# Folded Fourier mixing and channel mix: the opening laid out anew

## The chip, the cores and the metric

The kernel runs on one core of a Trainium2 chip. The metric is the device time in microseconds (us), the median of several runs. On the core, TensorE (PE, with PEld for its weight loads) multiplies matrices, VectorE (DVE) and ScalarE (ACT) compute on partitions, GpSimd (POOL) makes index tables and issues most of the loads here, and SyncE (SP) issues the stores. Each engine runs its own instructions in order.

## The reference

```python
def _attn_ref(x):                      # x: (8, 3072, 256)
    X = np.fft.fft(x, axis=1)
    X = np.fft.fft(X, axis=2)
    return X.real
def _moe_ref(x, mu_k, mu_r, w_k, w_v, w_r):   # d_model 256, d_ff 1024
    x_prev = x shifted by one row along the sequence, zeros first
    xk = mu_k * x + (1.0 - mu_k) * x_prev
    xr = mu_r * x + (1.0 - mu_r) * x_prev
    k = np.maximum(xk @ w_k, 0.0)
    v = k * k @ w_v
    r = 1.0 / (1.0 + np.exp(-(xr @ w_r)))
    return r * v
```

The output of the first function is the input of the second. All arrays are float32; the kernel works in float16 with float32 sums.

## The kernel before

There are 8 batches. The Fourier sum over the 3072 rows of a batch is split into a first stage of 96 rows on the partitions, and a second of 32 to 64. Since only the real part is wanted, x is folded with its mirror image: `fold` adds to the rows that a plain load brings (`load_p`, into an `xp` tile) the mirrored rows that a gather brings (`load_m`, into an `xm` tile, read backwards). A batch comes in two halves, h = 0 and 1; in the kernel before the first has eight slots q of 96 rows and the second nine. `load_xh` loads a half.

After the fold come, for the first batch and the first half of the second, `a_sum` (two products into one sum, evicted to tile `a`), and for the others `butterfly` on DVE and `a_item` on TensorE. `d_half` and `d_item` turn `a` into the shared tile `g_all` with the table `w_eo`, `c_item` multiplies `g_all` with the table `m_cs` into `pq`, and DVE makes `halves`, `diff` and `mix_part` (or `mix`) of it, which are the inputs of the channel mix. There a chunk of 512 tokens goes through `k_products` and a Relu eviction (`k_piece`, line 618), `square`, `v_tile`, `r_item` and `v_out`.

All tables are computed on the chip. `w_pm` comes from columns `one` (one value for each partition) and a sine on ScalarE. `m_cs` comes from some twenty DVE operations on columns `row`, from `angles` (`m_angles`, `m_wrap`) and sines (`m_sine`, two parts: tables 0 to 8 and 9 to 13, `NJ1` = 9), and `m_first` mends its first slice. `ueo`, made on GpSimd, is masked on DVE and becomes `w_eo`. `rows` makes the row numbers by which the weights are gathered, on GpSimd. `keep_busy` multiplies zeros on TensorE.

The order of the work is written out by hand and pinned on each engine (`pin_order`), so an instruction that waits holds back all that stand behind it on its engine. The opening (lines 668 to 730) handles the first batch. Then a loop of steps runs, one for each quarter of a chunk: in each step `k_piece`, the work that `at(step, ...)` put down for it, `v_tile`, `v_out` and `square`. Loads of batch 1 and the first weights are issued in `loads`, the mirrored weights in `loads_2`; all go through GpSimd's queue, in order.

PSUM has three slots of 1024 columns (`ps_w`) and two of 512 (`ps_v`), taken in turn.

Of the kernel before, what the change touches and what calls it, by code (L numbers as in the profile page):

```python
# [39 lines left out]
def kernel(  # L40
# [18 lines left out]
    NJ, NJ1 = 14, 9  # L59
# [49 lines left out]
    xm_sb = [const.tile([96, XM0 + 2049], FP16, name=f"xm{n}") for n in range(3)]  # L109
    idx_4 = const.tile([96, 4], UINT32)  # L110
# [7 lines left out]
    def load_p(b, h, q0, n):  # L118
        r = 0 if q0 == 8 else 8 * h + q0 + 1
        src = dataclasses.replace(x[b, r:r + 1, :], ap=[[32 * D, 96], [D, n], [1, D]])  # L120
        nc.gpsimd.dma_start(out=xp_t[b, h][:, q0:q0 + n], in_=src)  # L121
# [4 lines left out]
    def load_m(b, h, q0, n):  # L126
        if q0 == 8:
            o, idx = 1, idx_0[:, b:b + 1]
        elif n == 8:
            o, idx = XM0, idx_8[:, b, h:h + 1]  # L130
        else:
            o, idx = XM0 + 1024 - 256 * q0, idx_4[:, 2 * h + q0 // 4:2 * h + q0 // 4 + 1]
        gather(xm_t[b, h][:, o:o + 256 * n], x.rearrange("b (s r) d -> (b s) (r d)", r=n), idx)

    def load_xh(b, h):
        x_tiles(b, h)
        for q0, n in ((0, 8), (8, 1))[:1 + h]:
            load_p(b, h, q0, n)
            load_m(b, h, q0, n)

    def fold(b, h, q0=0, n=0):

        n = n or 8 + h
# [3 lines left out]
        o = XM0 + 1792 - 256 * q0  # L147
# [5 lines left out]
    def butterfly(b, h):  # L153
        n = 8 + h
# [53 lines left out]
    for xm in xm_sb:  # L208
        V.memset(xm[:, XM0 + 2048:XM0 + 2049], 0.0)
# [24 lines left out]

    pd_f = const.tile([P, 1], FP32)
    ueo = const.tile([P, 2, 2, 64], INT32)
    w_eo = const.tile([P, 2, 128], FP16)
    nc.gpsimd.tensor_scalar(out=pd_f, in0=pcol_i, scalar1=float(TURN) / D, scalar2=None,
                            op0=ALU.mult)
    for c in range(2):  # L240
        nc.gpsimd.tensor_scalar(out=ueo[:, :, c], in0=veo_i[:, :, c], scalar1=pd_f,
                                scalar2=0.75 * (1 - c) * TURN, op0=ALU.mult, op1=ALU.add)
    nc.gpsimd.iota(idx_8, pattern=[[S // 8, B], [-1, 2]], base=S // 8 - 1, channel_multiplier=-4)
# [12 lines left out]
    V.memset(m_cs, 0.0)  # L256
# [42 lines left out]
    for i in range(2):  # L299
# [3 lines left out]
    ts(ueo, ueo, TURN - 1, ALU.bitwise_and)  # L303
    par_i = const.tile([P, 1], INT32)
    ts(par_i, pcol_i, 1, ALU.bitwise_and)
# [4 lines left out]
    t64_i = const.tile([P, 1], INT32)  # L310
    ast = const.tile([P, 2 * NJ + 64], FP32)
    ast_i = const.tile([P, 64], INT32)
    row = {n: const.tile([P, 1], FP32, name=f"row_{n}")
           for n in ("s", "c", "z", "t", "t2", "q", "rr", "rs", "ph", "ph0", "phs", "sgn", "sg0",
                     "sgs", "to", "to0", "by")}
    ts(t64_i, pcol_i, 63, ALU.bitwise_and)
# [536 lines left out]
```

## Time and profile before

| | us |
|---|---|
| median of 3 runs | 458.45 (458.33 to 458.47) |
| profiled execution, its own time | 459.53 |
| its span, first to last instruction | 457.8 |
| PE busy | 428.6 (94%) |
| DVE busy | 363.2 (79%) |
| ACT busy | 325.1 (71%) |
| POOL busy | 61.9 (14%) |
| mean granted TensorE clock | 0.999 |

The page gives busy time by engine; most of the span lies in the loop of steps. The opening is read from the timeline: each row has the start and the length in us, engine, line, operation, output and inputs, count, and in brackets the idle time of the engine before it with what ended that. Where rows of a group are merged, the length is that of all of them, gaps within included.

### The profile page before, as it was taken

The page shows a single profiled execution, that of the slowest core. Times are in us where ns is not written, and L with a number is a line of the kernel's source. Part 1 is how long each engine was busy: PE and PEld are TensorE (multiplying, and loading weights), DVE is VectorE, ACT ScalarE, POOL GpSimd, SP SyncE. Part 2 cuts the span into 40 slices and gives each one's busy share as a digit, 9 for nine tenths or more (in the row PEclk, how much of TensorE's full clock was granted, in tenths as well). Part 3 has the DMA queues.
Part 4 walks back from the last instruction along what each step waited for, and adds up shares of the span by engine and source line. Part 5 has one row for each costly group of instructions (what it writes and reads, how often), then busy time and mean ns, then how long its engine had stood idle before and what let it go on. Part 6 is the DMA issues. An engine that isn't in the chain of part 4 may idle for free.

```text
span 457.8 us, 8433 instructions
## 1 busy us (share of the span) xinstructions
PE 428.6 (94%) x3433; PEld 307.2 (67%) x3433; DVE 363.2 (79%) x523; ACT 325.1 (71%) x369; POOL 61.9 (14%) x88
## 2 busy tenths in 40 slices
PE   3348899999999999999999999999999999999996
PEld 1234667767777777777777777777777777676764
DVE  3737999998879887898879887898879865997453
ACT  3147888777777777777777777777777777666661
POOL 7872324000400031000400030000000000000000
PEclk9999999999999999999999999999999999999999
DMA  7897566722852248222852244222222222222223
GB/s 110 129 164 122 77 140 108 156 48 69 152 127 55 69 87 178 71 52 64 149 129 54 70 87 107 70 55 63 69 64 54 70 69 48 70 68 70 71 69 93
DMA packets 35739, 40.93 MB, mean 89 GB/s; under 512 B 4082, under 2 KB 31732, under 8 KB 35700
## 3 DMA queue, kind: packets, MB, share of 16 engines
q1 hardware_dynamic: 27524, 25.05, 22.1%
q0 software_dynamic: 8016, 15.21, 21.4%
q8 instruction: 27, 0.44, 0.4%
q10 hardware_dynamic: 160, 0.13, 0.1%
q14 instruction: 12, 0.10, 0.1%
HBM read 30.41 MB, written 25.17 MB: 121 GB/s over the span
## 4 chain that ended last, share of the span: by engine, by line
PE 85%; DVE 6%; POOL 4%; issue 1%; DMA 1%; ACT 1%; POOLq 0%; DVEq 0%
PE psV L646 35%; PE psW L608 33%; PE psW L632 9%; PE psW L528 3%; PE psW L490 3%; PE psW L458 2%; DVE k L625 2%; DMA wv_sb<-in_moe_w_v_dram 1%; POOL xm L124 1%; DVE x L588 1%; DVE d L552 1%; DVE p L148 1%; POOL xp L121 1%; DVE o L656 0%; POOL wk L124 0%
## 5 line engine op out<-in xcount | busy, mean ns | idle before, releaser
L618 ACT ACTIVATE rl<-psW 128x1024 f16<-128x1024 f32 x192 | 196.0, 1023 | 97.9 <-PE psW L608 92.2
L646 PE MATMUL psV<-wv_sb,k 128*128 128x256 f16 x1536 | 199.3, 273 | 0.4 <-DVE k L625 0.2
L608 PE MATMUL psW<-x,wk 128*128 128x512 f16 (+1 forms) x776 | 196.8, 377 | 1.0 <-ACT rl L618 0.6
L646 PEld LDWEIGHTS <-k 128*128 128x128 f16 x1536 | 146.0, 98 | 28.7 <-DVE k L625 1.2
L625 DVE TENSOR_TENSOR k<-rl 128x2048 f16<-128x2048 f16 (+1 forms) x98 | 117.6, 1201 | 50.9 <-ACT rl L618 47.0
L608 PEld LDWEIGHTS <-wk 128*128 128x128 f16 x776 | 75.8, 98 | 51.3 <-issue 1.8
L656 DVE SCALAR_TENSOR_TENSOR o<-psV,r 128x512 f32<-128x512 f32 (+1 forms) x97 | 66.2, 682 | 15.5 <-PE psV L646 12.6
L577 DVE TENSOR_TENSOR x<-y,t 128x1536 f16<-128x1536 f16 x60 | 57.5, 958 | 2.1
L632 PE MATMUL psW<-wr,x 128*128 128x256 f16 x384 | 49.8, 273 | 0.0
L637 ACT ACTIVATE r<-psW 128x1024 f16<-128x1024 f32 x48 | 48.9, 1018 | 0.8 <-PE psW L632 0.8
L632 PEld LDWEIGHTS <-x 128*128 128x128 f16 x384 | 37.5, 98 | 14.6 <-issue 0.3
L121 POOL DMA_DIRECT2D xp<-in_x_dram x26 | 15.1, 580 | 200.5 <-DVE p L150 187.8
L438 ACT ACTIVATE a<-psW 128x832 f16<-128x832 f32 x31 | 26.6, 859 | 14.0 <-PE psW L475 14.0
L124 POOL DMA_INDIRECT xm<-in_x_dram,idx x26 | 30.9, 1187 | 7.8 <-issue 7.6
L438 ACT ACTIVATE pq<-psW 128x768 f16<-128x768 f32 (+5 forms) x34 | 28.6, 844 | 2.5 <-PE psW L528 2.3
L438 ACT ACTIVATE g_all<-psW 128x1024 f16<-128x1024 f32 (+3 forms) x39 | 28.1, 723 | 1.4 <-PE psW L490 1.4
L528 PEld LDWEIGHTS <-g_all 128*128 128x128 f16 (+1 forms) x233 | 15.2, 99 | 11.5 <-ACT g_all L438 3.3
L528 PE MATMUL psW<-m_cs,g_all 128*128 128x128 f16 (+2 forms) x233 | 19.2, 222 | 2.5 <-ACT g_all L438 2.3
L544 DVE TENSOR_TENSOR y<-pq 128x960 f16<-128x960 f16 (+5 forms) x38 | 18.6, 531 | 3.2 <-ACT pq L438 1.9
L148 DVE TENSOR_TENSOR p<-xp,xm 96x2048 f16<-96x2048 f16 (+3 forms) x18 | 20.8, 1155 | 0.1
L475 PEld LDWEIGHTS <-p 96*128 96x128 f16 x50 | 5.9, 130 | 22.1 <-DVE p L150 21.4
L564 DVE TENSOR_SCALAR t<-d,mu_m 128x1536 f16<-128x1536 f16 x32 | 19.7, 615 | 0.0
(118 smaller groups left out, 193.1 us busy)
## 6 DMA issues: line engine op xcount, KB each, us to landing
out_dram<-o SPq DMA_DIRECT2D x190, 128.0 KB, 2.4
xp<-in_x_dram POOLq DMA_DIRECT2D x14, 384.0 KB
xp<-in_x_dram POOLq DMA_DIRECT2D x4, 192.0 KB
wv_sb<-in_moe_w_v_dram POOLq DMA_DIRECT2D x1, 512.0 KB
xm<-in_x_dram,idx POOLq DMA_INDIRECT x26
xp<-in_x_dram POOLq DMA_DIRECT2D x8, 48.0 KB
out_dram<-o ACTq DMA_DIRECT2D x2, 64.0 KB
out_dram<-o SPq DMA_DIRECT2D x2, 64.0 KB
```

Source lines behind the costliest of these rows:

```text
L124: nc.gpsimd.indirect_dma_start(dst, None, src, bass.IndirectOffsetOnAxis(ap=idx, axis=0))
L148: V.tensor_tensor(out=p[:, q0:q0 + n], in0=xp[:, q0:q0 + n], in1=_v(xm, o + 256, [(-256, n), (-1, 256)]), op=ALU.add)
L438: nc.scalar.activation(out=out_ap, in_=in_ap, func=AF.Copy)
L528: nc.tensor.matmul(out=ps[0:m, o:o + 64 * k], lhsT=g_all[:, u, 128 * min(f, 1):128 * min(f, 1) + m], rhs=m_cs[:, f % 2, sl:sl + k], start= ...
L577: V.tensor_tensor(out=dst, in0=_v(y_t[b], 64 * (NSL * a + lo + 3 * m), [(1, n)]), in1=_v(x_t["t", a], 64 * lo, [(1, n)]), op=ALU.subtract ...
L608: nc.tensor.matmul(out=st["k", ds][:, 512 * hs + lo:512 * hs + hi], lhsT=wk_sb[m][a][:, 128 * fc:128 * fc + 128], rhs=xk[:, a, 512 * i + l ...
L618: nc.scalar.activation(out=st["rl"][:, 2 * ds:2 * ds + 2], in_=st["k", ds].rearrange("p (f t) -> p f t", f=2), func=AF.Relu, bias=0.0, sca ...
L625: V.tensor_tensor(out=k2_t[c][:, lo:hi], in0=r, in1=r, op=ALU.mult)
L632: nc.tensor.matmul(out=ps[:, 256 * tb:256 * tb + 256], lhsT=x_t[b, 1, m][:, a, 512 * i + 128 * tb: 512 * i + 128 * tb + 128], rhs=wr_sb[m] ...
L637: nc.scalar.activation(out=st["r", c], in_=ps, func=AF.Sigmoid)
L646: nc.tensor.matmul(out=st["v", tb - h][:, 256 * h:256 * h + 256], lhsT=k2_t[c][:, fc, 128 * tb:128 * tb + 128], rhs=wv_sb[:, fc], start=(f ...
L656: V.scalar_tensor_tensor(out=o.rearrange("p a b -> p (a b)")[:, 0:256 * n], in0=st["v", t0][:, 0:256 * n], scalar=16.0, in1=st["r", c][:, ...
```

## The change

The opening of the first batch is written anew, with small changes to every batch's loads:

- Loads. The first half of a batch now has nine slots and the second eight. The first batch comes by a nine-slot plain load, a one-slot gather, an eight-slot gather, an eight-slot plain load and two four-slot gathers, in place of ten transfers; the later batches by two plain loads and three gathers in place of three and three. In `a_item` and `a_sum` the second half takes slot 0 of the first half where it took its own slot 8, and batch 1 gets a one-slot `butterfly` for that.
- Index tables on GpSimd. One `ramp` replaces the ramps `k1c_i`, `kst_i` and `veo_i`; `rows` is six iotas in place of nine arithmetic operations, and all of it stands ahead of the weight gathers.
- Column constants. The DVE operations on `row` columns are replaced by memsets and ten operations on rows of one partition (`row_ramps`), which TensorE turns into eight columns by eight products with a 1x1 unit (`row_turn`), and `angle_parts`. `turn_table` becomes one operation, `m_first` one copy. The clearing of `m_cs` moves from DVE to ScalarE.
- Order. The table constants come before the first fold; the folds are of 5, 4, 4 and 4 slots. The sines of `m_cs` come in three parts, tables 0 to 4, 5 to 8 and 9 to 13 (`NJ1` = 5, `NJ2` = 9). The weights are loaded before batch 1. `diff` and `mix_part` are of four slices each, and the first `k_products` stand before `c_item` of slices 9 to 16, which uses the small PSUM slots.
- `keep_busy` is called with 14, 11, 5, 1 and 4 products in the opening, in place of one call with 2; the call with 10 at the start stays.

The diff, cut to its core:

```diff
-    NJ, NJ1 = 14, 9
+    NJ, NJ1, NJ2 = 14, 5, 9
...
-    def load_p(b, h, q0, n):
-        r = 0 if q0 == 8 else 8 * h + q0 + 1
+    def load_p(b, h):
+        r, n = 9 * h, 9 - h
         src = dataclasses.replace(x[b, r:r + 1, :], ap=[[32 * D, 96], [D, n], [1, D]])
...
-    def load_m(b, h, q0, n):
...
+    def load_m(b, h, o, n, idx):
+        gather(xm_t[b, h][:, XM0 + o:XM0 + o + 256 * n],
+               x.rearrange("b (s r) d -> (b s) (r d)", r=n), idx)
+    def load_m0(b):
+        load_m(b, 0, 2048, 1, idx_0[:, b:b + 1])
     def load_xh(b, h):
         x_tiles(b, h)
-        for q0, n in ((0, 8), (8, 1))[:1 + h]:
-            load_p(b, h, q0, n)
-            load_m(b, h, q0, n)
+        load_p(b, h)
+        if h == 0:
+            load_m0(b)
+        load_m(b, h, 0, 8, idx_8[:, b, h:h + 1])
     def fold(b, h, q0=0, n=0):
-        n = n or 8 + h
+        n = n or 9 - h
...
-        o = XM0 + 1792 - 256 * q0
+        o = XM0 + 256 * (8 - h - q0)
...
-        V.memset(xm[:, XM0 + 2048:XM0 + 2049], 0.0)
-    load_p(0, 0, 0, 4)
-    load_m(0, 0, 0, 4)
-    load_p(0, 0, 4, 4)
-    load_m(0, 0, 4, 4)
...
+        V.memset(_v(xm, XM0 + 2048, [(256, 2)]), 0.0)
+    load_p(0, 0)
+    iota(pcol_i, pattern=[[0, 1]], base=0, channel_multiplier=1)
+    iota(ramp, pattern=[[1, P]], base=0, channel_multiplier=0)
+    iota(idx_0, pattern=[[S, B]], base=S, channel_multiplier=-32)
+    iota(idx_0[0:1], pattern=[[S, B]], base=0, channel_multiplier=0)
+    load_m0(0)
+    iota(idx_8, pattern=[[S // 8, B], [-1, 2]], base=S // 8 - 1, channel_multiplier=-4)
+    load_m(0, 0, 0, 8, idx_8[:, 0, 0:1])
...
+    load_p(0, 1)
+    load_m(0, 1, 1024, 4, idx_4[:, 0:1])
+    load_m(0, 1, 0, 4, idx_4[:, 1:2])
...
-    V.memset(m_cs, 0.0)
     mu_rows(0)
+    nc.scalar.activation(out=m_cs.rearrange("p c s t -> p (c s t)").bitcast(FP32),
+                         in_=_v(zeros.bitcast(FP32), 0, [(0, 2 * NJ), (1, 64)]), func=AF.Copy)
...
+    for n, v0, v1, at, v in ((PH, 0.75, 0.0, 47, 0.75), (PHS, 0.5, 0.75, 15, 0.75),
+                             (PH0, 0.75, 0.5, 47, 0.75), (PHS0, 0.5, 0.25, 15, 0.25)):
...
+    def row_ramps():
+        one = ramp[0:1]
+        ts(rv(Q, 0, (32, 4), (1, 16)), _v(one, 1, [(0, 4), (1, 16)]), 0.0, ADD)
+        ts(rv(Q, 16, (32, 4), (1, 16)), _v(one, 1, [(0, 4), (1, 16)]), 32.0, ADD)
+        V.memset(rv(Q, 15, (32, 4)), 0.0)
+        ts(rv(Q2, 0, (1, P)), rv(Q, 0, (1, P)), 2.0, MUL)
...
+    def row_turn():
+        ps = ps_w()
+        for n in range(8):
+            nc.tensor.matmul(out=ps[:, n:n + 1], lhsT=rw[:, n], rhs=unit_1, start=True, stop=True)
+        ts(cols[:, 0:TO], ps[:, 0:TO], float(TURN) / S, MUL)
+        V.tensor_copy(out=cols[:, TO:TO + 2], in_=ps[:, TO:TO + 2])
...
-    ts(row["s"], t64_i, 47.0, ALU.is_equal, 32.0, MUL)
-    ts(row["z"], t64_i, 15.0, ALU.is_equal)
-    ts(row["c"], t64_i, 32.0, ALU.is_ge, -32.0, MUL)
-    ts(row["t"], t64_i, row["c"], ADD)
...
-    ts(ast_i, kst_i[:, NJ:NJ + 64], row["rr"], MUL, float(TURN) / R, MUL)
-    ts(ast_i, ast_i, TURN - 1, ALU.bitwise_and)
-    V.tensor_copy(out=ast[:, 2 * NJ:2 * NJ + 64], in_=ast_i)
-    for i, ph in ((0, "ph"), (1, "phs")):
-        ts(ast[:, NJ * i:NJ * i + NJ], kst_i[:, 0:NJ], row["rs"], MUL, row[ph], ADD)
+    def angle_parts():
+        ts(ast_i, ramp[:, 0:64], col(RR), MUL)
+        ts(ast_i, ast_i, TURN - 1, ALU.bitwise_and)
+        V.tensor_copy(out=ast[:, 2 * NJ:2 * NJ + 64], in_=ast_i)
+        for i in range(2):
+            ts(ast[:, NJ * i:NJ * i + NJ], ramp[:, 0:NJ], col(Q2), MUL, col(PH + i), ADD)
+        V.tensor_copy(out=_v(ast[hi64], 0, [(NJ, 2)]), in_=cols[hi64, PH0:PH0 + 2])
     def turn_table():
-        ts(row["to0"], row["c"], 2.0, MUL, row["s"], ADD)
-        ts(row["to"], row["z"], -32.0, MUL, row["to0"], ADD)
...
-        ts(turn, kst_i[:, NJ:NJ + 128], row["to0"], ALU.is_equal, row["sg0"], MUL)
+        ts(turn, ramp, col(TO), ALU.is_equal, col(SG), MUL)
...
     def rows():
-        late, low, f128 = [const.tile([P, 1], FP32, name=f"row{n}") for n in range(3)]
-        ts = nc.gpsimd.tensor_scalar
-        ts(out=late, in0=pcol_f, scalar1=64.0, scalar2=-127.0, op0=ALU.is_ge, op1=ALU.mult)
-        ts(out=low, in0=pcol_f, scalar1=2.0, scalar2=late, op0=ALU.mult, op1=ALU.add)
-        ts(out=row_i[:, 0:1], in0=low, scalar1=0.0, scalar2=None, op0=ALU.add)
...
+        for a in range(2):
+            for half in range(2):
+                iota(_v(row_i[64 * half:64 * half + 64], a, [(3 - 2 * a, 2)]), pattern=[[0, 2]],
+                     base=256 * a + half * (1 - 2 * a), channel_multiplier=2 - 4 * a)
+        iota(row_i[0:1, 2:3], pattern=[[0, 1]], base=0, channel_multiplier=0)
+        iota(_v(row_i[0:1], 1, [(2, 2)]), pattern=[[0, 2]], base=128, channel_multiplier=0)
...
     def m_first():
-        im = slice(96, 128)
-        nc.scalar.activation(out=m_cs[im, 0, 0], in_=m_cs[im, 0, 0], func=AF.Copy,
-                             scale=row["sgn"][im])
-        nc.scalar.activation(out=m_cs[hi64, 1, 0], in_=m_cs[hi64, 1, 0], func=AF.Copy,
-                             scale=row["sgs"][hi64])
-        V.memset(m_cs[hi64, :, 0, 0:1], 0.0)
+        nc.scalar.activation(out=_v(m_cs[hi64], 0, [(2 * NJ * 64, 2)]), in_=zeros[hi64, 0:2],
+                             func=AF.Copy)
     def loads():
-        load_xh(1, 0)
+        rows()
         for a in range(2):
-            next(row_part)
             gather(wk_sb[0][a], moe_w_k, row_i[:, a:a + 1])
         nc.gpsimd.dma_start(out=wv_sb, in_=moe_w_v.rearrange("(fc p) v -> p fc v", p=128))
+        load_xh(1, 0)
         for a in range(2):
             gather(wr_sb[0][a], moe_w_r, row_i[:, a:a + 1])
         load_xh(1, 1)
-        next(row_part)
...
+                for z, q, o, w in ((eo_t[b, 0], 0, 0, _v(w_pm[0:96], WA, [(1, WB)])),
+                                   (eo, 7, 1, _v(w_pm[0:96], 1, [(2, WB)]))):
+                    nc.tensor.matmul(out=_v(ps, 128 * i + o, [(2, WB)]), lhsT=z[:, q, e, :],
...
-    def a_sum(b, h, q0, eng="A", n=4):
+    def a_sum(b, h, i0, engs="A"):
...
+            n = 4 // len(engs)
+            if i % n == n - 1:
+                evac(_v(a_t[b], 8 * h + i0 + i + 1 - n, [(16, 2 * WA), (1, n)]),
+                     _v(ps, 256 * (i + 1 - n), [(1, 2 * WA), (256, n)]), engs[i // n])
...
-    def c_item(b, s0, n, eng="A", turn_late=False):
+    def c_item(b, s0, n, eng="A", turn_late=False, small=False):
-        ps = ps_w()
+        ps, bank = (ps_v(), 256) if small else (ps_w(), 512)
...
-    fold(0, 0, 0, 4)
-    a_sum(0, 0, 0)
+    keep_busy(14)
+    row_ramps()
+    row_turn()
+    angle_parts()
+    ts(ueo, ueo, TURN - 1, ALU.bitwise_and)
     eo_sine()
     eo_rest()
+    keep_busy(11)
+    fold(0, 0, 0, 5)
+    a_sum(0, 0, 0)
+    fold(0, 0, 5, 4)
+    a_sum(0, 0, 4)
+    loads()
     m_angles(0, NJ1)
-    fold(0, 0, 4, 4)
-    a_sum(0, 0, 4)
     m_wrap(0, NJ1)
+    m_sine(0, NJ1)
+    m_first()
+    mu_turn()
+    keep_busy(5)
     fold(0, 1, 0, 4)
     a_sum(0, 1, 0)
-    m_sine(0, NJ1)
-    m_first()
-    fold(0, 1, 4, 5)
-    loads()
-    a_sum(0, 1, 4, "V", 2)
-    a_sum(0, 1, 6, "A", 2)
-    mu_turn()
-    m_angles(NJ1, NJ)
+    fold(0, 1, 4, 4)
+    keep_busy(1)
+    m_angles(NJ1, NJ2)
+    a_sum(0, 1, 4, "VA")
+    m_wrap(NJ1, NJ2)
     d_half(0, 0, ps_v(), "A")
     d_half(0, 2, ps_v(), "V")
-    m_wrap(NJ1, NJ)
     c_item(0, 0, 5, "A", True)
     c_item(0, 5, 4, "A", True)
+    m_sine(NJ1, NJ2)
     d_item(0, 1)
     halves(0, 0, 5)
+    diff(0, 0, 4)
+    mix_part(0, 0, 0, 4)
     halves(0, 5, 9)
-    diff(0, 0, 8)
-    for lo, hi in ((0, 4), (4, 8)):
-        mix_part(0, 0, lo, hi)
-        if lo == 0:
-            keep_busy(2)
-            c_item(0, 9, 4, "A", True)
-            c_item(0, 13, 4, "A", True)
-            m_sine(NJ1, NJ)
-            k_products(chunks[0], 0, 0, 256)
-            k_products(chunks[0], 1, 0, 256)
+    keep_busy(4, ps_w())
+    k_products(chunks[0], 0, 0, 256)
+    k_products(chunks[0], 1, 0, 256)
+    diff(0, 4, 8)
+    mix_part(0, 0, 4, 8)
+    c_item(0, 9, 4, "A", True, True)
+    c_item(0, 13, 4, "A", True, True)
+    m_angles(NJ2, NJ)
+    m_wrap(NJ2, NJ)
+    m_sine(NJ2, NJ)
...
+    at(6, butterfly, 1, 0, 1)
```

More of the change, by code (lines that the diff above doesn't have):

```diff
@@ L108 @@
     XM0 = 257
-    xm_sb = [const.tile([96, XM0 + 2049], FP16, name=f"xm{n}") for n in range(3)]
-    idx_4 = const.tile([96, 4], UINT32)
+    xm_sb = [const.tile([96, XM0 + 2306], FP16, name=f"xm{n}") for n in range(3)]
+    idx_4 = const.tile([96, 2], UINT32)
     idx_8 = const.tile([96, B, 2], UINT32)
@@ L290 @@
                             (WA, 2, "n0", one["f2"]), (WA + 1, 2, "n2", one["f3"])):
-        ts(_v(u_w, o, [(step, NU)]), k1c_i, one[by], MUL, ph, ADD)
+        ts(_v(u_w, o, [(step, NU)]), ramp[:, 0:NU], one[by], MUL, ph, ADD)
     ts(u_w, u_w, TURN - 1, ALU.bitwise_and)
@@ L302 @@
     mu_rows(1)
[L303 to L310, printed above, removed]
     ast = const.tile([P, 2 * NJ + 64], FP32)
     ast_i = const.tile([P, 64], INT32)
[L313 to L316, printed above, removed]
```

140 lines of the change are left out of this document (54 added, 86 removed).

## The prediction

> **What bounds the kernel now.** I read the page first, then the stretches, then the opening in order of time.
>
> ```profile
> span 457.8 us, 8433 instructions
> PE 85%; DVE 6%; POOL 4%; issue 1%; DMA 1%; ACT 1%; POOLq 0%; DVEq 0%
> ```
>
> ```profile
> 2.00:9.00 7.00, 3.43 (x9) 0.91 (x6) 3.54 (x19) 2.49 (x13) 5.67 (x15) 1.00 0.89 128
> 2.00:15.00 13.00, 3.43 (x9) 0.91 (x6) 5.11 (x30) 2.49 (x13) 10.96 (x25) 1.00 0.91 131
> 15.00:28.00 13.00, 4.60 (x24) 3.11 (x24) 6.90 (x25) 6.37 (x10) 10.84 (x16) 1.00 0.89 133
> 40.00:45.00 5.00, 4.43 (x31) 2.61 (x30) 4.53 (x10) 4.96 (x7) 0.00 (x0) 1.00 0.50 96
> 45.00:50.00 5.00, 3.42 (x33) 2.04 (x31) 4.86 (x14) 3.81 (x7) 0.00 (x0) 1.00 0.00 0
> 50.00:60.00 10.00, 9.97 (x85) 7.36 (x83) 9.90 (x16) 9.26 (x11) 6.88 (x6) 1.00 0.76 105
> ```
>
> The columns are the stretch, its length, busy time (and count) of PE, PEld, DVE, ACT and POOL, the clock, the DMA share and GB/s. From 50 us on PE is full, so the rest of the program is a block of PE work that the change leaves alone. The change can win only what brings that block forward: the end moves by as much as the first Relu eviction (line 618), where the steady pipeline begins. Everything below is a sum up to that instruction, which starts at 41.89 us. The opening, from its timeline:
>
> ```profile
> 0.98 4.45 PE L181 MATMUL psV<-zeros 128*128 128x512 f16 x10 [0.98 <-DVE xm L209]
> 1.35 1.55 DVE L256 MEMSET m_cs<- 128x1792 uint32 x1 [0.33 <-issue]
> 2.82 0.10 DVE L279 CAST pcol_f<-pcol_i 128x1 f32<-128x1 int32 x1
> 4.45 0.95 POOL L124 DMA_INDIRECT xm<-in_x_dram,idx  x1 [0.30 <-issue]
> 5.44 0.24 DVE L276 TENSOR_SCALAR u_w<-u_w 128x156 int32<-128x156 int32 x1
> 10.76 0.94 POOL L124 DMA_INDIRECT xm<-in_x_dram,idx  x1 [0.30 <-issue]
> 13.23 0.29 DVE L276 TENSOR_SCALAR ueo<-ueo 128x256 int32<-128x256 int32 x1 [7.55 <-POOL ueo L241]
> 16.86 0.25 DVE L276 TENSOR_SCALAR ast_i<-kst_i,row_rr 128x64 int32<-128x64 int32 x1
> 17.68 0.30 DVE L276 TENSOR_SCALAR ast<-kst_i,row_rs,row_phs 128x14 f32<-128x14 int32 x1
> 17.89 0.68 DVE L148 TENSOR_TENSOR p<-xp,xm 96x1024 f16<-96x1024 f16 x1
> 20.44 0.86 ACT L438 ACTIVATE a<-psW 128x832 f16<-128x832 f32 x1 [12.92 <-PE psW L475]
> 24.87 2.53 ACT L389 ACTIVATE m_cs<-rl,m_pi 64x1152 f16<-64x1152 int32 x2
> 28.17 0.06 DVE L400 MEMSET m_cs<- 64x2 f16 x1 [5.86 <-DMA wv_sb<-in_moe_w_v_dram]
> 28.31 0.82 DVE L148 TENSOR_TENSOR p<-xp,xm 96x1280 f16<-96x1280 f16 x1
> 31.25 1.01 PE L202 MATMUL psW<-unit,mu_p 2*128 2x2 f32 x4
> 32.19 1.03 PE L490 MATMUL psV<-w_eo,a 128*128 128x128 f16 x8
> 33.49 1.91 PE L528 MATMUL psW<-m_cs,g_all 128*128 128x64 f16 x15 [0.26 <-issue]
> 34.60 1.44 ACT L438 ACTIVATE pq<-psW 128x640 f16<-128x640 f32 x2 [1.16 <-PE psW L528]
> 37.32 1.67 DVE L588 SCALAR_TENSOR_TENSOR x<-d,mu_f,y 128x256 f16<-128x256 f16 x4
> 37.45 1.02 ACT L438 ACTIVATE g_all<-psW 128x1024 f16<-128x1024 f32 x1 [1.41 <-PE psW L490]
> 40.32 1.67 ACT L389 ACTIVATE m_cs<-rl,m_pi 64x640 f16<-64x640 int32 x2
> 41.89 4.63 ACT L618 ACTIVATE rl<-psW 128x1024 f16<-128x1024 f32 x5
> 45.49 0.35 DVE L276 TENSOR_SCALAR turn<-kst_i,row_to,row_sg 128x128 f16<-128x128 int32 x1
> 48.28 1.22 DVE L148 TENSOR_TENSOR p<-xp,xm 96x2048 f16<-96x2048 f16 x1
> ```
>
> Two waits make the opening long. First, DVE idles 7.55 us for a GpSimd table (ueo, 13.23), then works through some twenty small column operations until 17.98, and the first fold starts behind them at 17.89 because DVE runs in order. Second, DVE idles 5.86 us before a memset at 28.17. The row names a DMA, but the memset writes m_cs behind ScalarE's m_first, and ScalarE spent 24.87 to 27.40 on nine tables' sines; the last fold (28.31) queues behind that memset. Neither wait is for x: batch 0 is 1.67 MB as it lands (two halves, each 96 x 8 rows of 512 B twice, and two pieces of one row more), and at the 131 GB/s of 2 to 15 us that is in by 2.0 + 12.8 = 14.8 us.
>
> **The change, step by step.** All starts in us.
>
> *To the first fold.* The m_cs memset (1.55 us) goes to ScalarE: bound 1.6 to 2.0 there, from 1.26 us per 1152 elements, hidden before w_pm, which waits for DVE's u_w anyway. It makes way for some 15 memsets of one row at about 0.06 us. So the column chain for w_pm starts at about 2.4 instead of 2.82 and ends at 5.2. Then ten operations on one partition (row_ramps): no such row exists; the nearest, 128x1 to 128x128 at 0.10 to 0.35 us, give 1.5 to 3.0; I take 2.0, so 7.2. TensorE now has 14 more dummy matmuls in front of row_turn. The row at 0.98 gives 0.43 us each, the row below 0.22:
>
> ```profile
> 42.94 1.93 PE L608 MATMUL psW<-x,wk 128*128 128x512 f16 x8 [0.57 <-ACT rl L618]
> 54.85 0.88 PE L475 MATMUL psW<-w_pm,p 96*128 96x208 f16 x8
> ```
>
> 14 x 0.22 to 14 x 0.43 is 3.1 to 6.0, from 5.43; I take 3.6 (a few slow ones, then fast), to 9.0, so these and not row_ramps gate row_turn. The trace shows the fast rate whenever TensorE is kept full (42.94 on) and the slow one in all broken work before 40 us; the clock column reads 1.00 in both, so it does not show there. [...]
>
> row_turn is eight fp32 matmuls of one column: 8 x 0.25 (1.01 for four at 31.25, slow clock) is 2.0 at most, 1.0 if the clock is double; I take 1.5, to 10.5. Two copies from PSUM with their wait 0.5 (0.16 for such a copy, the rest handover), angle_parts 1.3 (five such operations took 16.86 to 17.98, and one small copy more), the ueo mask 0.29: the first fold starts at 12.6 instead of 17.89. ueo itself must be there: GpSimd makes it after four iotas and two gather issues (0.95 each), some 7 us, hidden by 5 us. The x it needs, 0.88 MB as one load and two gathers, is in by 2.0 + 0.88/0.128 = 8.9 at the 2-to-9 rate, a cover of 3.7 us; the whole of batch 0 as above by 14.8.
>
> *To d_half.* fold of 5 rows 1.0 (0.82 and its small second operation), to 13.6; a_sum 0.9 (row at 54.85); second fold to 14.45, its a_sum to 15.4, ScalarE eviction 0.86, to 16.3. The 11 dummies fill 10.5 to 12.9 and cost nothing at the fast rate. DVE does five tables' angles and mask, 0.84 + 0.48 by the rows below, to 15.8, then waits for mu_turn (four fp32 matmuls, 15.4 to 16.4) and copies mu_f, to 16.65:
>
> ```profile
> 32.38 0.84 DVE L381 TENSOR_TENSOR rl<-ast 128x640 int32<-128x640 f32 x1
> 33.87 0.48 DVE L276 TENSOR_SCALAR rl<-rl 128x640 int32<-128x640 int32 x1
> 30.32 0.59 DVE L436 CAST a<-psV 128x416 f16<-128x416 f32 x1 [0.97 <-PE psV L475]
> 31.36 0.55 ACT L438 ACTIVATE a<-psV 128x416 f16<-128x416 f32 x1 [3.25 <-PE psV L475]
> ```
>
> Behind that new wait stand the folds of the second half, 16.65 to 17.5 and to 18.35. They no longer wait for sines: m_first is now one two-element copy, and ScalarE's sines of five tables (1.67) run 16.3 to 18.0 beside them. a_sum(0,1,0) 17.55 to 18.5 behind five dummies, evicted by 19.4; the last a_sum 18.6 to 19.7, its halves evicted by DVE (0.59) and ScalarE (0.55), the latter to 20.3. d_half starts at 20.35 against 32.19: 11.8 us won.
>
> *To the first Relu.* c_item at 21.65 (1.30 later, as before), its evictions on ScalarE 22.75 to 24.2, four tables' sines 1.4 (0.83 x 512/640, twice), the d_item eviction 1.0, to 26.6; then four k products of 256 columns that wait for their PSUM slot (0.4 to 0.9 by the rate, I take 0.5) and c_item 9 (0.6), to 27.7; its eviction and the next 1.2, to 28.9; the last five tables' sines 1.67, to 30.5. DVE beside it: halves, diff and mix_part of four slices to 25.4, the other four to 27.3, the last angles and mask to 28.6, just ahead of the sines that need them. So the first Relu starts at 30.5 instead of 41.89: 11.4 us won. Part of the table work that ScalarE was late with is now merely behind the evictions, so 0.4 us of the 11.8 is given back.
>
> *Later.* turn_table falls from six operations (44.44 to 45.84) to the one of 0.35, in a stretch where DVE is busy 4.86 of 5 us: worth 0 to 1.0. The extra butterfly of one row at step 6 adds two operations, 0.2 to 0.4. I take 0.6 net. Per batch, one plain load fewer, and the nine-row and eight-row halves change places: the same elements, nothing. In the loads, weights now go ahead of batch 1: w_k is in after 1.67 + 0.52 MB, 2.0 + 2.19/0.132 = 18.6, wanted at 25.4; batch 1's first half after 3.6 MB, at 29.3, wanted by fold(1,0) at 48.28 - 12 = 36.3.
>
> **Sum:** 11.4 + 0.6 = 12.0 us. The profiled execution took 459.53 us, so 447.5; the median of the runs shown is 458.45, 1.1 below it, which gives 446.5.
>
> **Rivals.**
>
> *The dummies stay slow* (they come before every step that they are meant to speed up). 14 end at 11.4, row_turn at 13.4, the fold starts at 15.5; the 11 end at 18.1 and hold back the a_sums, now 1.6 each, to 21.3; mu_turn and five dummies to 24.5, the last a_sum to 28.4, d_half at 29.0: only 3.2 us won, 455.3. For it: no fast matmul is in the trace before 40 us. Against it: there TensorE always had pauses, here it has hardly any.
>
> *x becomes the bound.* A fold now waits for a gather of eight rows, not four. At the full rate it is covered; at the 96 GB/s of a window such as 40 to 45 the batch lands at 19.4 instead of 14.8, the last fold (17.5) starts 1.9 later: 448.4, and 450 if the lag is doubled by gathers issued late.
>
> *Slower than before:* batch 1's first half, issued at 13.28 before, now stands behind 1.05 MB of weights, and fold(1,0) at step 4 stands in DVE's order ahead of the squares that TensorE's v products need. It costs something once the queue runs under 3.6/34.3 = 105 GB/s, and more than the change wins under 3.6/46.3 = 78 GB/s; at 70 it lands at 53.4, 5.1 after the old fold: 463.6. GpSimd must write each transfer beside a busy DVE, and one of its operations took 1.38 beside a DVE operation that ends with it, against 0.29 alone:
>
> ```profile
> 17.71 0.29 POOL L365 TENSOR_SCALAR row<-pcol_f 128x1 f32<-128x1 f32 x1
> 18.70 1.38 POOL L367 TENSOR_SCALAR row<-row 128x1 f32<-128x1 f32 x1
> ```
>
> [...] Against the rival: 131 and 133 GB/s in two long stretches, with DVE busy in the second.
>
> *The gain is given back:* if the block after 42 us were set by a later DMA and not by PE, nothing would move, 458. Against it: 9.97 of 10 us of PE.
>
> **How the numbers follow.** Forecast 0.70, 443 to 449.5 (all unknown costs at their low ends, 1.0 + 0.5 + 0.6 + 0.4, more of the turn table, 3.5 in all; at their high ends 3.0). Late x 0.12 (448 to 451.5), slow dummies 0.10 (451 to 456), given back 0.03, slower 0.05. Leaving out the last three and the forecast's own tails, the range is 443.0 to 451.5. A change of 0.2%, 0.9 us, is about what a measurement here can tell from none: faster 0.92, same 0.03, slower 0.05.
>
> **What would show it.** Right: row_turn at about 9 to 10.5, first fold at 12 to 13.5, no wait of DVE over 2 us after it, d_half near 20.4, first Relu near 30.5, PE full from about 38, later stages unchanged in length. Wrong: dummies at 0.43 us beyond 8 us; folds released by a DMA; DVE stalled at fold(1,0); a stage behind 40 us longer than its twin before.

## The result and the profile after

The changed kernel takes 446.6 us (median of 4 runs, 446.18 to 447.0) against 458.46 for the kernel before on the same chip: ratio 0.9738, interval 0.9721 to 0.9755. The forecast was 446.5, range 443.0 to 451.5. The profiled execution took 446.77 with a span of 445.0.

In the changed kernel the fold is line 147, the Relu eviction 607, a_sum 462, the dummies 180, row_turn 297, d_half 479 and c_item 517. Its opening, from the timeline (start, length, engine, line, operation; gaps within a merged group are included):

```profile
0.98 7.85 PE L180 MATMUL psV<-zeros 128*128 128x512 f16 x24 [0.98 <-DVE xm L208]
4.85 0.24 DVE L315 TENSOR_SCALAR u_w<-u_w 128x156 int32<-128x156 int32 x1
5.66 0.15 PEld L180 LDWEIGHTS <-zeros 128*128 128x128 f16 x1 [0.28 <-issue]
6.08 2.26 PEld L180 LDWEIGHTS <-zeros 128*128 128x128 f16 x11 [0.27 <-issue]
6.23 0.49 DVE L315 TENSOR_SCALAR rw<-ramp 1x64 f32<-1x64 int32 x3
8.76 1.94 PE L297 MATMUL psW<-unit,rw 1*128 1x1 f32 x16
10.74 0.16 DVE L315 TENSOR_SCALAR cols<-psW 128x6 f32<-128x6 f32 x1 [4.02 <-PE psW L297]
12.61 0.82 DVE L147 TENSOR_TENSOR p<-xp,xm 96x1280 f16<-96x1280 f16 x1
14.62 1.66 ACT L425 ACTIVATE a<-psW 128x832 f16<-128x832 f32 x2 [1.08 <-PE psW L462]
15.95 0.16 DVE L203 COPY mu_f<-psW 128x4 f32<-128x4 f32 x1 [0.26 <-PE psW L201]
16.03 0.69 DVE L147 TENSOR_TENSOR p<-xp,xm 96x1024 f16<-96x1024 f16 x1
16.31 1.68 ACT L382 ACTIVATE m_cs<-rl,m_pi 64x640 f16<-64x640 int32 x2
16.84 0.68 DVE L147 TENSOR_TENSOR p<-xp,xm 96x1024 f16<-96x1024 f16 x1
19.15 0.70 PE L462 MATMUL psW<-w_pm,p 96*128 96x208 f16 x6 [0.70 <-DVE a L423]
20.48 0.62 PE L479 MATMUL psV<-w_eo,a 128*128 128x128 f16 x8 [0.63 <-ACT a L425]
21.57 1.22 PE L517 MATMUL psW<-m_cs,g_all 128*128 128x64 f16 x15 [0.47 <-ACT g_all L425]
26.98 1.13 ACT L425 ACTIVATE pq<-psV 128x512 f16<-128x512 f32 x2 [1.11 <-PE psV L517]
28.13 1.66 ACT L382 ACTIVATE m_cs<-rl,m_pi 64x640 f16<-64x640 int32 x2
29.70 4.63 ACT L607 ACTIVATE rl<-psW 128x1024 f16<-128x1024 f32 x5
32.25 0.34 DVE L315 TENSOR_SCALAR turn<-ramp,cols 128x128 f16<-128x128 int32 x1
35.39 1.35 DVE L147 TENSOR_TENSOR p<-xp,xm 96x2304 f16<-96x2304 f16 x1
```

The stretches, in the columns of before:

```profile
2.00:15.00 13.00, 12.48 (x64) 6.45 (x62) 8.40 (x45) 5.26 (x18) 10.57 (x23) 1.00 0.90 142
15.00:28.00 13.00, 10.24 (x94) 6.58 (x92) 9.36 (x23) 9.71 (x15) 9.93 (x11) 1.00 1.14 184
38.00:48.00 10.00, 9.90 (x81) 7.02 (x79) 9.88 (x18) 9.14 (x12) 5.13 (x4) 1.00 0.76 114
```

Read down the starts: first fold 12.61 (before 17.89), d_half 20.48 (32.19), first Relu 29.70 (41.89), fold(1,0) 35.39 (48.28), and TensorE is full from 38 us on, 12 us earlier than before. From the first Relu to the end of the span it is 415.3 us, before 415.9, so the gain lies ahead of the first Relu but for 0.6 us. The two long waits of DVE are gone. The 4.02 us at 10.74 are new: DVE's rows are ready at 6.72, and TensorE turns them only when its dummies end at 8.83.

### The profile page after: what moved, and what is told of

Read it like the earlier page. It is cut to its first block, busy times and chain, and to the rows that moved or that the text cites. A ratio compares the mean times of both kernels' runs of the same rounds, so it can differ in the third digit from the quotient of the medians.

```text
span 445.0 us, 8512 instructions
## 1 busy us (share of the span) xinstructions
PE 433.1 (97%) x3482; PEld 309.2 (69%) x3482; DVE 361.4 (81%) x529; ACT 326.6 (73%) x371; POOL 54.6 (12%) x69
## 4 chain that ended last, share of the span: by engine, by line
PE 85%; DVE 5%; DMA 4%; POOL 3%; issue 1%; ACT 1%; POOLq 0%
PE psV L635 36%; PE psW L597 34%; PE psW L621 9%; DMA xp<-in_x_dram 2%; PE psW L479 2%; PE psW L517 2%; PE psW L445 2%; DMA wr<-in_moe_w_r_dram,row_i 1%; DVE k L614 1%; POOL xm L124 1%; DVE x L577 1%; POOL wk L124 1%; DVE d L541 1%; DVE p L147 1%; DVE o L645 1%
## 5 line engine op out<-in xcount | busy, mean ns | idle before, releaser
L124 POOL DMA_INDIRECT xm<-in_x_dram,idx x25 | 32.6, 1305 | 8.0 <-issue 6.7
L121 POOL DMA_DIRECT2D xp<-in_x_dram x16 | 9.1, 569 | 193.5 <-DVE p L149 184.4
L425 ACT ACTIVATE a<-psW 128x832 f16<-128x832 f32 (+1 forms) x32 | 27.1, 850 | 1.9 <-PE psW L462 1.9
L425 ACT ACTIVATE pq<-psW 128x768 f16<-128x768 f32 (+5 forms) x32 | 27.4, 859 | 1.3 <-PE psW L517 1.3
L147 DVE TENSOR_TENSOR p<-xp,xm 96x2304 f16<-96x2304 f16 (+3 forms) x18 | 20.8, 1156 | 0.0
L479 PEld LDWEIGHTS <-a 128*128 128x128 f16 x208 | 14.1, 98 | 8.1 <-ACT a L425 0.9
L517 PE MATMUL psW<-m_cs,g_all 128*128 128x128 f16 (+2 forms) x221 | 17.4, 218 | 1.2 <-ACT g_all L425 1.2
```

Of the source, the lines that this page charges most:

```text
L124: nc.gpsimd.indirect_dma_start(dst, None, src, bass.IndirectOffsetOnAxis(ap=idx, axis=0))
L147: V.tensor_tensor(out=p[:, q0:q0 + n], in0=xp[:, q0:q0 + n], in1=_v(xm, o + 256, [(-256, n), (-1, 256)]), op=ALU.add)
L425: nc.scalar.activation(out=out_ap, in_=in_ap, func=AF.Copy)
L517: nc.tensor.matmul(out=ps[0:m, o:o + 64 * k], lhsT=g_all[:, u, 128 * min(f, 1):128 * min(f, 1) + m], rhs=m_cs[:, f % 2, sl:sl + k], start= ...
```

## The experiments

A ratio is the mean of a kernel's runs against the mean of the kernel before, run beside it on the same chip. The chips differed (medians of the kernel before from 458.46 to 460.21 us), so ratios are compared, and in brackets stands what a ratio saves of 458.46 us. Expectations in us are read the same way. Each interval is about 0.0016 to either side (0.7 us) where nothing else is said.

**Two lines of order in the old kernel.** The first takes the ueo mask (line 303) and its sine out of the way of the columns:

```diff
-    ts(ueo, ueo, TURN - 1, ALU.bitwise_and)
...
     fold(0, 0, 0, 4)
     a_sum(0, 0, 0)
-    eo_sine()
-    eo_rest()
     m_angles(0, NJ1)
     fold(0, 0, 4, 4)
     a_sum(0, 0, 4)
+    ts(ueo, ueo, TURN - 1, ALU.bitwise_and)
+    eo_sine()
+    eo_rest()
```

> The kernel before with one edit: the mask of ueo (line 303) and its sine move behind the first two folds, so that DVE's twenty column operations start at 5.7 us and not at 13.4 behind GpSimd. Nothing of the loads, of the rows on TensorE or of the dummies. Theory (the first wait was this order): the first fold starts at 10.3 instead of 17.89, the last at about 20.3 instead of 28.31, the time falls by 7 to 8.5: 450 to 451.5. Rival (the new loads or the turn by TensorE carry the gain): within 1 us of 458.4.

Measured: ratio 0.9833 (7.7 us; 450.8). From its timeline, the first fold, the last one and the first Relu:

```profile
10.03 0.68 DVE L148 TENSOR_TENSOR p<-xp,xm 96x1024 f16<-96x1024 f16 x1
...
21.38 0.06 DVE L399 MEMSET m_cs<- 64x2 f16 x1 [5.85 <-ACT m_cs L397]
21.52 0.82 DVE L148 TENSOR_TENSOR p<-xp,xm 96x1280 f16<-96x1280 f16 x1
...
34.44 4.63 ACT L617 ACTIVATE rl<-psW 128x1024 f16<-128x1024 f32 x5
```

The first fold starts 7.9 us earlier and the first Relu 7.45. The last fold, at 21.52, comes 1.2 us later than expected. Here the profile names what the memset waits for: ScalarE's m_first (line 397). In the profile before, the same wait of 5.86 us was put down to a load of w_v; that was the wrong name, as the prediction read it. The second edit takes the sines behind the evictions:

```diff
     a_sum(0, 1, 0)
-    m_sine(0, NJ1)
-    m_first()
     fold(0, 1, 4, 5)
...
     a_sum(0, 1, 6, "A", 2)
+    m_sine(0, NJ1)
+    m_first()
     mu_turn()
```

> As the run before, and the sines of the first nine tables with m_first move behind the evictions of the last a_sum, so that the last fold no longer stands behind m_first's memset. Theory (both waits were order): last fold at 15 to 16, c_item near 22 instead of 33.49, 446.5 to 448.5, nearly the whole gain of the change without its rows, loads or dummies. Rival (the ten old transfers bound x): the last fold waits for a load until 17 or later, 449 or more.

Measured: ratio 0.9764, interval 0.9747 to 0.9780 (10.8 us).

```profile
15.53 0.82 DVE L148 TENSOR_TENSOR p<-xp,xm 96x1280 f16<-96x1280 f16 x1
...
22.80 0.06 DVE L399 MEMSET m_cs<- 64x2 f16 x1 [4.33 <-ACT m_cs L397]
...
23.41 1.94 PE L527 MATMUL psW<-m_cs,g_all 128*128 128x64 f16 x15 [2.62 <-ACT g_all L437]
...
31.42 4.63 ACT L617 ACTIVATE rl<-psW 128x1024 f16<-128x1024 f32 x5
```

So two moves in the order, with the old loads, no row on TensorE and no dummies added, save 10.8 of the 12.0 us; the two intervals overlap, so this pair alone does not show that the rest of the change adds to it. x did not hold the last fold: at 15.53 no wait stands in front of it. c_item comes at 23.41, 1.4 us later than expected, since the moved sines now stand ahead of an eviction that it waits for. From c_item to the first Relu it is 8.0 us here, 8.4 before and 8.1 in the changed kernel, so no gain shows from what the change reorders there (diff and mix_part by four slices, `k_products` ahead of `c_item`).

**How the columns are made.** The eight columns of the changed kernel by DVE operations on columns, in place of row memsets, row_ramps and row_turn:

```diff
     keep_busy(14)
-    row_ramps()
-    row_turn()
+    columns()
+    ps_n["W"] += 1
     angle_parts()
```

`columns` makes six of the eight by 22 operations, 21 of them on one column each, as before the change; the other two, for the turn table, are made by five operations just ahead of it, as before. The second new line leaves the order of the PSUM slots as it was.

> The changed kernel with the same eight columns made by 21 DVE operations on columns, as before the change, in place of the row memsets, row_ramps and row_turn; order, loads and dummies as changed (ratio of the changed kernel 0.9738). Theory (what counts is that the columns no longer stand behind ueo, not how they are made): 21 operations at 0.2 us from about 4.9 end at 9.3, angle_parts and the mask at 11.1, the first fold at 11.1 to 11.4 instead of 12.61: ratio 0.970 to 0.972. Rival (TensorE's turn frees DVE of work that would be late): first fold at 13 or later, ratio 0.9745 or more.

In this first form the column q had another value in slot 31 than the changed kernel has, which makes values of the table, and so the output, wrong, but changes no operation's size. Measured: ratio 0.9715, interval 0.9693 to 0.9737 (13.1 us), first fold at 10.52. With q as in the changed kernel, two operations fewer:

> As e5_columns (columns by DVE, ratio 0.9715, first fold at 10.52), with slot 31 of the column q as the changed kernel has it, which is two operations fewer. Theory (how the columns are made does not matter, only that nothing stands ahead of them): first fold at 10.1 to 10.4, ratio 0.969 to 0.972, at or below the changed kernel's 0.9738. Rival (rows turned by TensorE are worth something by themselves): ratio 0.9745 or more.

Measured: ratio 0.9701, interval 0.9685 to 0.9717 (13.7 us).

```profile
10.27 0.82 DVE L147 TENSOR_TENSOR p<-xp,xm 96x1280 f16<-96x1280 f16 x1
...
14.35 0.69 DVE L147 TENSOR_TENSOR p<-xp,xm 96x1024 f16<-96x1024 f16 x1 [0.58 <-DMA xm<-in_x_dram,idx]
...
28.63 4.63 ACT L636 ACTIVATE rl<-psW 128x1024 f16<-128x1024 f32 x5
```

The turn by TensorE does not bring the first fold forward: the old kind of column work, no longer behind ueo, is done 2.3 us sooner than the turn behind 14 dummies, and no later than the turn behind 4 (10.31, below). It is worth something later, since it makes the two columns of the turn table too: from the first Relu to fold(1,0) it is 6.39 us in this run (28.63 to 35.02), as before the change (6.39), and 5.69 in the changed kernel. The row at 14.35 shows the next bound: the second half's first fold now waits 0.58 us for a gather.

**The dummies.** First all five calls out (14, 11, 5, 1 and 4 products; the PSUM slots are still taken in the same turn):

```diff
-    keep_busy(14)
...
-    keep_busy(11)
...
-    keep_busy(5)
...
-    keep_busy(1)
...
-    keep_busy(4, ps_w())
```

> The changed kernel without its five calls of dummy products (14, 11, 5, 1, 4); the ten at the start stay. Theory (the gain is the order of DVE's and ScalarE's work, the dummies only keep TensorE at its fast rate): row_turn starts at 6.75 us instead of 8.76 but takes 4.0 instead of 1.94 at the slow rate (0.25 per pass, as the old mu_turn), so the first fold stays near 12.6; then every a_sum pair costs 1.6 instead of 0.9, mu_turn 1.0 instead of 0.6, and the first Relu comes 3 to 4.5 us later: 449.5 to 451. Rival (the dummies carry the gain): the opening falls back to the slow case of the prediction, 455 or more. Rival (the dummies are dead weight in front of row_turn): 446.6 or less.

Measured: ratio 0.9781, interval 0.9765 to 0.9797 (10.0 us).

```profile
5.00:10.00 5.00, 2.53 (x18) 1.93 (x16) 3.29 (x20) 1.79 (x9) 4.30 (x8) 0.91 0.89 132
10.00:15.00 5.00, 3.69 (x20) 3.05 (x20) 2.98 (x6) 2.35 (x5) 4.32 (x10) 0.50 0.96 172
15.00:20.00 5.00, 3.25 (x19) 2.64 (x19) 3.22 (x8) 2.89 (x5) 3.78 (x6) 0.50 0.91 122
25.00:30.00 5.00, 4.00 (x26) 2.19 (x24) 4.03 (x10) 3.00 (x5) 3.65 (x4) 0.54 1.12 212
```

```profile
6.36 1.72 PE L297 MATMUL psW<-unit,rw 1*128 1x1 f32 x14 [0.16 <-DVE rw L285]
...
10.22 0.82 DVE L147 TENSOR_TENSOR p<-xp,xm 96x1280 f16<-96x1280 f16 x1 [0.27 <-issue]
11.31 2.96 PE L462 MATMUL psW<-w_pm,p 96*128 96x208 f16 x16 [3.23 <-DVE p L149]
...
32.06 4.63 ACT L607 ACTIVATE rl<-psW 128x1024 f16<-128x1024 f32 x5
```

The first fold comes at 10.22, 2.4 us earlier than with the dummies: row_turn, 0.4 us behind the ten at the start, was not slowed (fourteen of its sixteen instructions took 1.72 us, all sixteen 1.94 in the changed kernel). Then TensorE pauses, the granted clock (the last column but two) is 0.50 from 10 us to nearly 30, sixteen products of a_sum take 2.96 us where the changed kernel takes 1.68, and the first Relu is 2.4 us late. So the first fourteen cost 2.4 us and the whole set gives back 4.8. The first theory had that part wrong: it took row_turn to be slow, and its loss was less than it said (448.4 by the ratio, where it had 449.5 to 451; the first Relu 2.4 us late, where it had 3 to 4.5). Then 4 in place of 14:

```diff
-    keep_busy(14)
+    keep_busy(4)
```

> The changed kernel with 4 dummies ahead of row_turn instead of 14. Its rows were ready at 6.72 us and TensorE's dummies ran until 8.83. Theory (the dummies gate row_turn, x is not yet a bound): row_turn starts at 6.75, the first fold at 10.6 instead of 12.6, the first Relu 1.5 to 2 us earlier: 444.6 to 445.1. Rival (x is the bound just behind): the folds are held by the landing of batch 0, whose second half is in at about 14, and the gain is under 0.7: 446 to 446.6. Rival (the rate falls back without the ten dummies): row_turn and the a_sums slow, 447 or more.

Measured: ratio 0.9687, interval 0.9671 to 0.9703 (14.3 us; 444.1, just under the first theory's 444.6 to 445.1).

```profile
6.21 1.94 PE L297 MATMUL psW<-unit,rw 1*128 1x1 f32 x16
...
10.31 0.81 DVE L147 TENSOR_TENSOR p<-xp,xm 96x1280 f16<-96x1280 f16 x1
...
28.01 4.63 ACT L607 ACTIVATE rl<-psW 128x1024 f16<-128x1024 f32 x5
```

The turn starts 2.55 us earlier and takes 1.94 as with fourteen, the clock column of this execution stays at 1.00, the first fold follows by 2.3 and the first Relu by 1.7. The dummies gated the turn, and x did not hold this fold.

**The loads.** Batch 0 in nine transfers:

```diff
-    load_p(0, 0)
+    load_p(0, 0, 0, 5)
...
-    load_m(0, 0, 0, 8, idx_8[:, 0, 0:1])
...
+    load_m(0, 0, 1024, 4, idx_4[:, 0:1])
+    load_p(0, 0, 5, 4)
+    load_m(0, 0, 0, 4, idx_4[:, 1:2])
...
-    load_p(0, 1)
-    load_m(0, 1, 1024, 4, idx_4[:, 0:1])
-    load_m(0, 1, 0, 4, idx_4[:, 1:2])
+    load_p(0, 1, 0, 4)
+    load_m(0, 1, 1024, 4, idx_4[:, 2:3])
+    load_p(0, 1, 4, 4)
+    load_m(0, 1, 0, 4, idx_4[:, 3:4])
```

> The changed kernel with batch 0 in nine transfers instead of six (the eight-slot gather as two, both plain loads as two). Theory (x is in before the folds want it, so the loads bring nothing): first fold at 12.6 as before this edit, weights some 3 us later and still in time, ratio 0.9725 to 0.9755. Rival (the fewer, larger loads carry a part): the second half's folds, at 16.03 and 16.84 in the changed kernel, wait for a load, 1 to 3 us later, ratio 0.976 to 0.980.

Measured: ratio 0.9751, interval 0.9735 to 0.9767 (11.4 us), inside the first theory's range; but its trace shows the rival's wait:

```profile
17.67 0.69 DVE L147 TENSOR_TENSOR p<-xp,xm 96x1024 f16<-96x1024 f16 x1 [1.48 <-DMA xm<-in_x_dram,idx]
...
31.20 4.63 ACT L610 ACTIVATE rl<-psW 128x1024 f16<-128x1024 f32 x5
```

The last fold waits 1.48 us for a gather, and the first Relu is 1.5 us later, though this execution's first fold was 0.7 us earlier (its dummies ran fast from 4.2 us on, those of the changed kernel from 6.1). Of the 1.5, 0.7 are there at d_half (21.16 against 20.48); the rest came behind it, where TensorE was slow for a while: the mean clock of 20 to 25 us is 0.66, and d_half took 1.01 us instead of 0.62. Whether that slow stretch follows from the wait is not shown. The times are not told apart (the intervals of 0.9738 and 0.9751 overlap), so in these openings the fewer loads are worth 0.7 to 1.5 us, not nothing, but in the time no gain of theirs is shown. The order of the later loads, as before the change:

```diff
     def loads():
+        load_xh(1, 0)
         rows()
...
-        load_xh(1, 0)
```

> The changed kernel with batch 1's first half issued ahead of w_k and w_v, as before the change. Theory (the loads' order does not set the first k products): w_k's two gathers are issued some 4 us later and land at about 22 (1.67 + 0.88 + 0.52 MB, 142 GB/s until 15 us and 184 after, the rates of the changed kernel), wanted at 24.7: ratio 0.9725 to 0.9755. Rival (with the opening shorter, w_k ahead of batch 1 is needed): the first k products wait for a gather 1 to 4 us, ratio 0.976 to 0.982.

Measured: ratio 0.9731 with an interval of 0.9693 to 0.9770, since its runs fell into two groups (446.4 and 446.5; 449.2 and 449.6). This decides nothing on the sum. In the profiled execution, one of the longer ones, the first k products start at 24.70 as in the changed kernel (24.71), so w_k was not late, against the rival. The loss is later: ScalarE's two evictions of c_item, at 26.98 and right behind it in the changed kernel, come at 27.63 and 29.07, the second after 0.85 us idle that the profile puts down to the k products; DVE sits 1.71 us idle before 29.70 with nothing named, and the first Relu starts at 31.27. What that was stays open.

**The table in three parts.** Two parts instead (`NJ1` = 9, the middle calls gone):

```diff
-    NJ, NJ1, NJ2 = 14, 5, 9
+    NJ, NJ1, NJ2 = 14, 9, 9
...
-    m_angles(NJ1, NJ2)
-    m_wrap(NJ1, NJ2)
-    m_sine(NJ1, NJ2)
```

> The changed kernel with the first nine tables' angles and sines in one part (NJ1 = 9), so the table comes in two parts as before. Theory (sines no longer hold back a fold, so the third part only moves ScalarE's 0.9 us from one place to another): DVE's angles of nine tables end 0.8 later, the folds of the second half start at 16.8 instead of 16.03, d_half 0.7 later, and 1.45 of sines are gone between c_item's and d_item's evictions: ratio 0.9725 to 0.9755. Rival (the split is what takes the sines off the path): first Relu 1.5 or more later, ratio 0.977 or more.

Measured: ratio 0.9723, interval 0.9707 to 0.9739 (12.7 us), just under the first theory's range; first Relu at 29.91 against 29.70. The third part makes no difference that these runs can tell.

**What the runs point to.** Four dummies before the turn, the last a_sum evicted by ScalarE alone (the changed kernel's TensorE waits 0.70 us there, at 19.15), and the last sines behind the fourth Relu:

```diff
-    keep_busy(14)
+    keep_busy(4)
...
-    a_sum(0, 1, 4, "VA")
+    a_sum(0, 1, 4, "A")
...
-    m_sine(NJ2, NJ)
+    at(3, m_sine, NJ2, NJ)
```

> The changed kernel with 4 dummies ahead of row_turn instead of 14 (e2_fill4: ratio 0.9687), the last a_sum evicted by ScalarE alone, and the last five tables' sines behind the fourth Relu instead of ahead of the first. In the changed kernel TensorE waited 0.70 us in that a_sum for DVE's eviction of the same PSUM tile, and ScalarE was full from 26.98 to 34.3 us. Theory (the chain to the first Relu sets the end): d_half 0.5 and the first Relu 2.1 us earlier than in e2_fill4, of which 1.2 to 2 stay: ratio 0.9645 to 0.966. Rival (ScalarE is the bound of that stretch as a whole, so a moved sine only moves the wait to the k squares or c_item 17): 0.5 or less, ratio 0.9675 to 0.969.

Measured: 444.19 us, ratio 0.9660, interval 0.9643 to 0.9677 (15.6 us): faster than the kernel before and, by intervals that do not overlap, than the changed one.

```profile
18.25 0.62 PE L479 MATMUL psV<-w_eo,a 128*128 128x128 f16 x8 [0.97 <-ACT a L425]
...
25.82 3.77 ACT L607 ACTIVATE rl<-psW 128x1024 f16<-128x1024 f32 x4
...
29.61 1.66 ACT L382 ACTIVATE m_cs<-rl,m_pi 64x640 f16<-64x640 int32 x2
31.31 1.02 ACT L607 ACTIVATE rl<-psW 128x1024 f16<-128x1024 f32 x1
```

d_half comes at 18.25, as in the run with 4 dummies (18.28), not 0.5 earlier. The a_sum edit did win its 0.5: from the first fold of the second half to d_half it is 3.93 us here (14.32 to 18.25) and 4.44 there (13.84 to 18.28). But that fold came 0.48 later here, because the eleven dummies behind the turn took 4.23 us, where they had taken 2.55, and held back the first a_sum (12.08 against 11.39):

```profile
8.01 4.23 PE L180 MATMUL psV<-zeros 128*128 128x512 f16 x11
...
5.00:10.00 5.00, 5.00 (x27) 3.00 (x26) 3.30 (x20) 1.79 (x9) 4.30 (x8) 0.83 0.84 129
```

The clock column reads 0.83 in that stretch, though TensorE was busy for all of it; in the run with 4 dummies it reads 1.00. So four dummies ahead of the turn held the fast rate through the opening in one profiled execution and not in the other; what decides it, these runs do not show. The first Relu is 2.2 us earlier than there, and 1.2 us of that stay in the time, by the ratios, whose intervals overlap; the rest is paid back by the sines at 29.61.

## Why the prediction was right

Its steps against the trace of the changed kernel, in us:

| step | predicted | measured |
|---|---|---|
| end of the w_pm columns | 5.2 | 5.09 |
| rows ready | 7.2 | 6.72 |
| dummies end | 9.0 | 8.83 |
| row_turn takes | 1.5 | 1.94 |
| first fold | 12.6 | 12.61 |
| second a_sum evicted | 16.3 | 16.28 |
| folds of the second half | 16.65 and 17.5 | 16.03 and 16.84 |
| d_half | 20.35 | 20.48 |
| c_item | 21.65 | 21.57 |
| first Relu | 30.5 | 29.70 |
| won later, on to fold(1,0) | 0.6 | 0.70 |

What was right is the reading of the two waits, and with it the mechanism. Two order edits alone in the old kernel save 10.8 us, so the causes named, ueo ahead of the columns and m_first ahead of the last fold, are shown and not only argued. That x, before, was no bound is shown by the same runs. The 0.6 us later is the turn table: with its five operations back, in the second run with DVE columns, the 0.70 is gone. Not tested by itself is GpSimd's rewritten work, by which ueo is ready at 7.25 instead of 13.19.

Four terms were mis-sized. row_turn took 1.94 us, not 1.5: the prediction took the four instructions at 31.25 for four products, where they are two, so its eight products are sixteen instructions, and its upper bound of 2.0 was too low at the price of 0.25 that it used; they took 0.12 each. The dummies ended 0.17 sooner than forecast and the work behind the turn took 0.2 less, so these errors cancel, and that the first fold came within 0.01 us of 12.6 is luck. mu_turn costs 0.60 us at the fast rate, not 1.0, which is most of the 0.6 by which the second half's folds came earlier; the last a_sum lost 0.70 of it again to a wait that the prediction did not have, TensorE behind DVE's eviction of half the same PSUM tile. From d_half on, ScalarE's evictions at the fast rate of TensorE came 0.4 to 0.8 sooner than the rows of before gave, since there they had waited for slow products (two c_item evictions in 1.19 instead of 1.44). Together the span fell by 12.8 and not by 12.0. The median still came out at 446.6: the profiled execution of before lay 1.1 above the median that the forecast went by, and that of the changed kernel only 0.2 above (446.77). So two errors of nearly a microsecond cancelled, and the agreement of the median to 0.1 us is luck.

The loads were priced at nothing because x would be in by 14.8. That cover was thinner than it said: what the first fold of the second half needs comes at 14.3 in the run with DVE columns, where the fold waited for it, and by 13.84 in the run with 4 dummies, where it did not; with nine transfers the last piece comes at 17.6. The rival "x becomes the bound" was thus near, some 2 us away at the fold of 16.03.

The rival with slow dummies failed as the prediction argued: TensorE, busy from 0.98 us on, sped up at 6.08 in the changed kernel. What the prediction said for this rival, that no fast product is in the trace before 40 us, was a wrong reading: twelve products of c_item took as long there as at 26.35 in the changed kernel (1.12).

```profile
38.53 1.13 PE L528 MATMUL psW<-m_cs,g_all 128*128 128x128 f16 x12 [1.31 <-ACT g_all L438]
```

In the changed kernel the weight loads of the dummies come 0.43 us apart until 6.08 (0.15 and an idle 0.28), then eleven in 2.26 us. In the trace of before all ten dummies are slow (4.45 us), so the few slow ones in the prediction's 3.6 us for the fourteen, and its 8 us for dummies still slow, were the author's estimate: no row showed when they would turn fast. The change came at 6.1, and the fourteen ended at 8.83 where it had 9.0. That a full TensorE is always fast, as the prediction read it, is not shown: in the last experiment it was busy for all of 5 to 10 us, and the eleven dummies behind the turn took 4.23 us.

What the prediction had for a GpSimd slowed by DVE was one operation of 1.38 us against one of 0.29. The 0.29 (at 17.71) was not alone, since a DVE operation of 0.30 starts at 17.68, and in the same trace a gather's issue took 0.95 beside the u_w operations (4.45) and 0.94 beside an idle DVE (10.76). The changed kernel does not settle whether DVE slows a gather's issue. Of two like ones, the first stands beside small column operations and the second, slower one beside the folds; but the third stands beside mix_part (25.86 to 26.74), and it is as fast as the first.

```profile
11.38 0.99 POOL L124 DMA_INDIRECT wk<-in_moe_w_k_dram,row_i  x1
12.67 1.59 POOL L124 DMA_INDIRECT wk<-in_moe_w_k_dram,row_i  x1 [0.30 <-issue]
...
25.77 0.95 POOL L124 DMA_INDIRECT wk<-in_moe_w_k_dram,row_i  x1 [0.89 <-DMA xp<-in_x_dram]
```

The slow one costs 0.6 us of GpSimd's time and nothing of the end, since w_k was in time. The slower rival, fold(1,0) late behind the weights, did not come near: the fold at 35.39 had no wait before it, and the DMA engines moved 142 GB/s until 15 us and 184 from there to 28, where the prediction's threshold was 105.

## What to carry to other kernels

On an engine that runs in order, look for the short instruction that waits: here a mask and a two-element memset, 0.35 us of work between them, held back 10.8 us. Price such a change by following one chain of starts to the instruction from which the rest is a block, and put every new item that is meant to help (here dummies ahead of a turn) on that same chain, since the help can hold back the very work that it is for. Check the name that a profile gives to a long wait against the order of the program before believing it.

## What was not expected of the hardware

The clock column can be silent. In the profile of before it reads 1.00 throughout, yet eight a_sum products take 1.57 us there at 18.84 and 0.88 at 54.85:

```profile
18.84 1.57 PE L475 MATMUL psW<-w_pm,p 96*128 96x208 f16 x8 [13.41 <-DVE p L150]
```

The trace says why: its first record of the clock is at 37.09 us, and the column reads 1.00 for time without a record. In the changed kernel the first record is at 6.07, where its dummies turn fast. Other executions of the kernel before, beside the last two experiments, list mean clocks of 0.963 to 0.966 in six of seven, as 31 to 34 us at the clock of 0.50 that the run without dummies shows would give (an estimate), and 0.999 in one; their times are close (459.5 to 460.4 and 459.24), so the 0.999 is no sign of a fast opening. Rates were a better witness than the column.

In the changed kernel an fp32 product of one column counts as two instructions (eight calls, sixteen in the row at 8.76), about 0.12 us each.
